# Retention followed by a multiplicative feed-forward layer: five moves in the order of transposes, state products and loads

## The chip, the cores and the metric

The kernel runs on one core of one Trainium2 chip. TensorE (PE, with its weight loads listed apart as PEld), VectorE (DVE), ScalarE (ACT) and GpSimd (POOL) each work through their own instruction list in program order; SyncE (SP) issues the transfers. The metric is the device time of one execution in microseconds, lower is better. Before the change seven executions have a median of 184.77 us (183.8 to 185.63).

## The reference

Inputs q, k and v are float32 of 4 batches x 8 heads x 768 positions x 64; the weights are w1 and w2 (512 x 1024), w3 (1024 x 1024) and w_out (1024 x 512). The output is 3072 x 512, float32.

```python
gamma = 1.0 - 2.0 ** (-5.0 - np.arange(H))          # one decay for each head
for t in range(S):
    state = gamma * state + outer(k[:, :, t], v[:, :, t])
    y[:, :, t] = q[:, :, t] @ state / sqrt(D)
x = y.transpose(0, 2, 1, 3).reshape(B * S, H * D)    # 3072 x 512
out = ((x @ w1) * (x @ w2)) @ w3 @ w_out
```

## The kernel before

**The mathematics as tiled.** The recurrence is cut into chunks of 128 positions: within a chunk, masked scores of queries and keys times the values (`intra`), and a product of the queries with the state before it (`inter`); the state itself is carried on with a product of keys and values (`kv`) and a decay. The decays are put into scalings of the values (`VS`), the outputs (`YS`) and the state (`GS`). All of these matmuls are 64 x 64 tiles in float16. The product w3 @ w_out is formed once (`W3O`), so that a chunk's feed-forward part is two products with W1 and W2 (`ab(f)`, f from 0 to 7: `a_unit`, four matmuls copied out of PSUM by ACT, and `b_unit`, four matmuls multiplied by that on DVE into `HT`) and two output blocks `o_unit(e)` of eight matmuls of 512 columns each.

**Stages.** The instruction order on each engine is the order of the program text (a manual schedule). At the start the weights arrive; `w3_transpose`, `w3_part` and `W3Block` (its eight matmuls are issued in portions by `mm(n)`, its result goes out by `back()`) form `W3O`. Meanwhile the first 256 positions of two batches are handled by two objects `Pairs`, b0 and b1, and W1 and W2 are cast to float16 as they land (`cast_w` and single copies). The first feed-forward block f0 is done by weight rows (`by_rows`), so that each W tile is used when it is there; `f1` fills in between. Then come steps m = 2 to 11 (so the "third step" is m = 2, the "fourth" m = 3, the "tenth" m = 9), each for one chunk of a pair of batches: `step2()` for m = 2, `step(m)` after it. A step holds the attention part of chunk m, the outputs of chunk m-1 and the feed-forward of chunk m-1 and m-2.

**Keys and queries, transposed.** The scores want keys and queries with the head dimension on partitions. Queries from step 4 on are transposed by transfers that SP issues (`q_dma`). Keys are transposed either on PE (`k_transposes`: eight 128 x 128 transposes into one PSUM bank and a DVE copy) or by such a transfer (`k_dma`); the set `K_PE` = (3, 5, 8) names the steps m in which the next step's keys go through PE.

**The order in a step before.** In `step(m)` for m > 4 the small matmuls stand together: `intra(m-1)`, `kv(m)`, `scores(m)`, `inter(m-1)`, the last held behind a one-element mark on ACT (`ended`) since two row halves add to one bank. For m in `EARLY` the `intra` stands earlier, among the `ab`. For m = 3 and 4 the order is another: step 3 has `inter(2)` and `scores(3)`, and later, among the `ab`, `intra(3)` and `kv(3)`; step 4 has `inter(3)`, `kv(4)`, `scores(4)`. After the group come, on DVE, the outputs of chunk m-1 (`outputs_back`, three operations), the evacuations of the state products (`kv_back`), and the masks on the scores (`am_back`).

**Memory that sets waits.** PSUM has eight banks: X0, X1, Y0, Y1 by name, and four in rotation (`ps_f`) for everything called psF, psO, psW and psK. Loads land in 22 staging tiles in rotation; the loads of q, k and v for steps 2 to 4 are issued at the top of the program in the order of the text, the later ones in the steps.

Of the kernel before, what the change touches and what calls it, by code (L numbers as in the profile page):

```python
# [18 lines left out]
def kernel(  # L19
# [11 lines left out]
    nc = tc.nc  # L31
# [9 lines left out]
    TB = 256  # L41
    K_PE = 4

# [43 lines left out]
    def load_k(m):  # L87
        load_kv(m, k_in, k)

    def load_v(m):  # L90
        load_kv(m, v_in, v)
# [39 lines left out]
    w1_st = [load_rows(moe_w1, d) for d in range(4)]  # L131
# [2 lines left out]
    load_q(3)  # L134
    for m in range(2, 5):
        load_k(m)
        if m == 3:
            load_q(4)
            load_q(5)
        load_v(m)  # L140

    Z = const.tile([128, 512], HP, name="zeros")
    nc.vector.memset(Z[:, :].bitcast(FP), 0.0)  # L143
# [136 lines left out]
    def q_cast(n, *engs):  # L280
        if n not in q_in:
            return
        q16s[n] = att.tile([128, 1024], HP, tag="q16", name="q16", bufs=2)
        pairs_cast(q16s[n], q_in.pop(n), *engs)
# [21 lines left out]
    def v_cast(m, engs):  # L306
        v16 = att.tile([128, 2, 512], HP, tag="v16", name="v16", bufs=3)
        v32 = v_in.pop(m)
        for e, eng in enumerate(engs):
            eng.tensor_tensor(  # L310
                v16[:, e, :].rearrange("j (h d) -> j h d", d=D),
                v32[:, e, :].rearrange("j (h d) -> j h d", d=D),
                VS[:, 2, :].unsqueeze(2).broadcast_to((128, H, D)),
                MULT,
            )
        v16s[m] = v16
# [19 lines left out]
    def q_dma(n):  # L336
        if n not in q16s:
            return
        qT = att.tile([128, 2, NP, 128], HP, tag="qT", name="qT", bufs=5)
        nc.sync.dma_start_transpose(  # L340
            qT[:, :, :, :].rearrange("p t a i -> p (t a) i"), q16s.pop(n)[:, :]
        )
        qTs[n] = qT
# [5 lines left out]
    def k_transposes(m, tag):  # L349
        k16, kT = k16s[m], new_kT(m)  # L350
        if tag:
            ps = bank(tag, [128, 2, NP, 128], HP, "psTk")
        else:
            ps = ps_f.tile([128, 2, NP, 128], HP, tag="psF", name="psTk")
        for e in range(2):
            for p in range(NP):
                nc.tensor.transpose(ps[:, e, p, :], k16[:, e, p * 128 : (p + 1) * 128], ident16[:, :])  # L357
        nc.vector.tensor_copy(
            kT[:, :, :, :].rearrange("p e a j -> p (e a j)"), ps[:, :, :, :].rearrange("p e a j -> p (e a j)")
        )  # L360
# [36 lines left out]
    class Pairs:  # L397
# [59 lines left out]
        def kv(self, psf):  # L457
            if psf:
                self.s = [ps_f.tile([128, NP, L], FP, tag="psF", name="psK") for s in range(2)]
            else:  # L460
                self.s = [bank(f"X{s}", [128, NP, L], FP, "psK") for s in range(2)]
            for p in range(NP):
                for t in range(2):
                    for s in range(2):
                        for r in range(2):
                            c0 = p * 128 + r * 64
                            nc.tensor.matmul(
                                self.s[s][half(r), p, :],
                                lhsT=self.k16[half(s), t * 512 + c0 : t * 512 + c0 + 64],
                                rhs=self.v16[half(s), t, c0 : c0 + 64],  # L470
                                start=(p == 0 and t == 0), stop=(p == NP - 1 and t == 1),
                            )
# [33 lines left out]
        def outputs_back(self, s):  # L506
            if self.e not in XT:
                XT[self.e] = xpool.tile([128, NP * 2, 2, L], HP, tag="xt", name="xt")
            nc.vector.tensor_tensor(
                XT[self.e][:, :, :, :].rearrange("p (a s) b x -> p a s (b x)", s=2)[:, :, s, :]  # L510
                .rearrange("p a (b i t) -> p a t b i", b=2, t=2),
                self.y[s][:, :, :].rearrange("p a (t b i) -> p a t b i", t=2, b=2),
                YS[:, 0:2, :, :].rearrange("p b a (t i) -> p a t b i", t=2), MULT,
            )
# [107 lines left out]
    class Ffn:  # L622
# [27 lines left out]
            ps = self.mm(W2, f)  # L650
            nc.vector.tensor_tensor(self.HT[:, f, :], self.pa.pop(f)[:, :], ps[:, :], MULT)  # L651

        def o_unit(self, e, parts=((0, 512),), store=True):
            bp, c = divmod(self.m, NCH)
            osb = fsb.tile([128, DM], FP, tag="osb", name="osb", bufs=4)
            r0 = (bp * 2 + e) * S + c * C if self.m > 1 else self.m * S + e * C
            for c0, c1 in parts:
                cs = slice(c0, c1)
                psO = ps_f.tile([128, c1 - c0], FP, tag="psF", name="psO")
                for f in range(8):  # L660
                    nc.tensor.matmul(  # L661
                        psO[:, :], lhsT=self.HT[:, f, e * 128 : (e + 1) * 128], rhs=W3O[f][:, cs],
                        start=(f == 0), stop=(f == 7),
                    )
                nc.scalar.activation(osb[:, cs], psO[:, :], AF.Copy, scale=final_scale)  # L665
                if store:
                    (nc.sync if self.m < NSTEP - 1 else nc.scalar).dma_start(out[r0 : r0 + 128, cs], osb[:, cs])
            return lambda: nc.sync.dma_start(out[r0 : r0 + 128, :], osb[:, :])
# [6 lines left out]
    def cast_w(W, st, d, on_dve):  # L675
        cast_to(W[d][:, :], st[d][:, :], on_dve)
# [46 lines left out]
    wb = W3Block(4)  # L723
# [5 lines left out]
    wb = W3Block(5)  # L729
# [4 lines left out]
    b0, b1 = Pairs(0), Pairs(1)  # L734
    b0.k_cast(nc.vector)
    q_transposes(0, "Y0", False)
    b0.k_transposes("Y1", True)
    b0.v_cast(nc.gpsimd, 0)
    b0.v_cast(nc.gpsimd, 1)
    wb = W3Block(6)  # L740
    wb.mm(4)
    am_back = b0.scores(0)
    am_back(0)
    am_back(1)
    wb.mm(4)
    wb.back()
    wb = W3Block(7)
    am_back = b0.scores(1)
    am_back(0)
    b0.kv(True)  # L750
# [15 lines left out]
    nc.scalar.copy(W1[0][:, 0:512], w1_st[0][:, 0:512])  # L766
    nc.gpsimd.tensor_copy(W1[0][:, 512:1024], w1_st[0][:, 512:1024])
    b1.v_cast(nc.gpsimd, 1)
    wb.mm(2)
    am_back = b1.scores(0)  # L770
    am_back(0)
    am_back(1)
    wb.mm(4)
    wb.back()
    cast_w(W1, w1_st, 1, False)
    b0.next_state_decay()
    nc.gpsimd.tensor_copy(W1[2][:, :], w1_st[2][:, :])
    nc.scalar.copy(W1[3][:, 0:512], w1_st[3][:, 0:512])
# [62 lines left out]
    for f in range(2):  # L841
        f1.ab(f)
    q_transposes(3, "Y0", False)
    stores = [f0.o_unit(0, store=False)]
    k_transposes(2, "Y1")
    f1.ab(2)

    def step2():
        am_back = scores(2)
        am_back(0)  # L850
        am_back(1)
        stores.append(f0.o_unit(1, store=False))
        k_cast(3, (nc.gpsimd, nc.scalar))
        for n in (4, 5):
            q_cast(n, nc.gpsimd)
        for n in (4, 5):
            q_dma(n)
        for store in stores:
            store()
        for f in range(3, 5):  # L860
            f1.ab(f)
        intra(2)
        kv_back = kv(2, True)
        kv_back(0)
        f1.ab(5)
        k_transposes(3, None)
        f1.ab(6)
        kv_back(1)
        v_cast(3, (nc.gpsimd, nc.gpsimd))
        f1.ab(7)  # L870

    EARLY = (6, 11, 12)

    K_PE = (3, 5, 8)

    def step(m):

        kv_backs = []  # L880
        if m > 4:
            last = None if m in EARLY else ended(intra(m - 1))
            if m < NSTEP:
                kv_backs.append(kv(m, True))
                am_back = scores(m)
            inter(m - 1, last)
        else:
            inter(m - 1)
            if m == 4:
                kv_backs.append(kv(m, True))  # L890
            am_back = scores(m)
        outputs_back(m - 1, 0)
        outputs_back(m - 1, 1)
        if m >= NSTEP:
            return
        if m + 1 < NSTEP:
            k_cast(m + 1, (nc.gpsimd, nc.gpsimd))
            if m not in K_PE:
                k_dma(m + 1)
        for kv_back in kv_backs:  # L900
            kv_back(0)
            kv_back(1)
        am_back(0)
        am_back(1)
        ffn[m - 2].o_unit(0)
        ffn[m - 2].o_unit(1)
        load_q(m + 3) if m % 2 == 0 else None
        load_k(m + 2)
        load_v(m + 2)
        load_q(m + 3) if m % 2 else None  # L910
        for f in range(2):
            ffn[m - 1].ab(f)
        if m + 1 in EARLY:
            intra(m)
        if m + 1 < NSTEP:
            v_cast(m + 1, (nc.gpsimd, nc.gpsimd))
        if m == 3:
            intra(m)
            kv_back = kv(m)
            kv_back(0)  # L920
        ffn[m - 1].ab(2)
        ffn[m - 1].ab(3)
        if m == 3:
            kv_back(1)
        if m % 2 == 0:
            for n in (m + 2, m + 3):
                q_cast(n, nc.gpsimd)
            for n in (m + 2, m + 3):
                q_dma(n)
        for f in range(4, 8):  # L930
            if f == 6 and m in K_PE:
                k_transposes(m + 1, None)
            ffn[m - 1].ab(f)
# [42 lines left out]
```

## Time and profile before

| what | value |
|---|---|
| median of 7 executions | 184.77 us |
| the profiled execution, its own time | 184.4 us |
| its span in the profile | 182.5 us |
| TensorE's granted clock, mean | 1.00 |
| matmuls, PE | 2642 |
| from HBM, read and written | 29.36 MB and 6.29 MB |
| mean duration of a 128 x 256 product with W1 or W2 on PE | 273 ns (x672) |
| mean duration of one output matmul of 512 columns on PE | 380 ns (x184) |
| mean duration of one key transpose on PE | 219 ns (x40) |
| DVE copy of eight transposed blocks | 691 ns (x5) |
| POOL, scaling one half of a step's values | 1044 ns (x20) |
| one transpose of keys by SP's queue: time on SP, time to landing | 1.24 to 2.43 us, 3.1 to 5.2 us (x5) |

A duration on PE is that of one matmul from start to end; matmuls follow one another before the one ahead has ended, so the distance between two starts is what a row of them costs. In the chain of waits each piece is listed with its start, its length and what it is; in the timeline each row has the start, the length, the engine and line, and in brackets how long the engine was idle before it and what ended that. A weight load on PEld belongs to the matmul that follows it.

### The profile page before, as it was taken

What the parts mean: (1) busy time and instruction counts of PE and PEld (TensorE: products, weight loads), DVE (VectorE), ACT (ScalarE), POOL (GpSimd) and SP (SyncE); (2) the same over time, 40 slices, a digit from 0 to 9 for tenths busy, and PEclk for the clock granted to TensorE, in tenths of its full rate; (3) what the DMA queues carried; (4) which work ended last, traced back from release to release, by engine and by line L of the source; (5) the groups of instructions that cost most, each with busy time, mean ns of one, the idle gap of its engine ahead of it and who ended that gap; (6) DMA issues with size and microseconds to landing.
All of it is one profiled execution on the core that took longest, in us unless ns stands there. A gap on an engine that the chain in (4) does not pass through costs nothing.

```text
span 182.5 us, 6235 instructions
## 1 busy us (share of the span) xinstructions
PE 175.7 (96%) x2642; PEld 125.2 (69%) x2642; DVE 109.4 (60%) x205; ACT 72.1 (39%) x156; POOL 71.0 (39%) x126
## 2 busy tenths in 40 slices
PE   7889989999999999999999999999999999999992
PEld 2445646588756795885877858769678587685872
DVE  2247668660669678649377493595684856846330
ACT  4353836565720342433424415243244242442532
POOL 3127536764547741824426364147362160000000
PEclk9999999999999999999999999999999999999999
DMA  5999999999999998999999999999999910200203
GB/s 207 355 418 403 299 288 347 403 374 245 206 274 223 164 304 179 200 306 203 216 224 200 307 171 243 199 243 251 170 170 271 166 66 4 115 0 22 96 0 115
DMA packets 78474, 39.44 MB, mean 216 GB/s; under 512 B 56304, under 2 KB 72944, under 8 KB 78448
## 3 DMA queue, kind: packets, MB, share of 16 engines
q1 hardware_dynamic: 78016, 38.54, 88.6%
q8 instruction: 20, 0.33, 0.8%
q10 hardware_dynamic: 432, 0.52, 0.8%
q14 instruction: 6, 0.05, 0.1%
HBM read 29.36 MB, written 6.29 MB: 195 GB/s over the span
## 4 chain that ended last, share of the span: by engine, by line
PE 78%; SPq 9%; DMA 8%; ACT 2%; issue 0%; DVE 0%; ACTq 0%
PE psF L636 40%; PE psO L661 23%; SPq L63 9%; DMA stg<-in_moe_w_out_dram 5%; DMA stg<-in_moe_w_dram 4%; PE psF L791 3%; PE psY L531 2%; PE psA L383 2%; PE psY L599 2%; PE psG L636 2%; PE psK L551 2%; PE psTk L357 1%; ACT w L220 1%; PE psTq L328 0%; ACT osb L665 0%
## 5 line engine op out<-in xcount | busy, mean ns | idle before, releaser
L636 PE MATMUL psF<-xt,w 128*128 128x256 f16 x672 | 77.0, 273 | 0.0
L636 PEld LDWEIGHTS <-w 128*128 128x128 f16 x704 | 68.2, 98 | 10.3
L651 DVE TENSOR_TENSOR ht<-pa,psF 128x256 f16<-128x256 f32 x88 | 36.9, 420 | 37.3 <-PE psF L636 31.7
L645 ACT COPY pa<-psF 128x256 f32<-128x256 f32 x80 | 29.8, 372 | 38.0 <-PE psF L636 38.0
L661 PE MATMUL psO<-w3o,ht 128*128 128x512 f16 (+2 forms) x200 | 43.7, 371 | 0.0
L661 PEld LDWEIGHTS <-ht 128*128 128x128 f16 x200 | 18.5, 98 | 19.7
L665 ACT ACTIVATE osb<-psO 128x512 f32<-128x512 f32 (+2 forms) x25 | 14.5, 580 | 44.2 <-PE psO L661 44.2
L614 DVE TENSOR_TENSOR xt<-psY,YS 64x512 f16<-64x512 f32 (+1 forms) x29 | 21.0, 726 | 4.4 <-PE psY L599 4.1
L310 POOL TENSOR_TENSOR v<-stg,VS 128x512 f16<-128x512 f32 x20 | 20.6, 1044 | 5.3 <-DMA stg<-in_v_dram 5.2
L303 POOL CAST k<-stg 128x512 f16<-128x512 f32 x18 | 11.1, 614 | 23.1 <-DMA stg<-in_k_dram 22.8
L290 POOL CAST q<-stg 128x1024 f16<-128x1024 f32 (+1 forms) x12 | 12.1, 1005 | 15.3 <-DMA stg<-in_q_dram 11.4
L566 POOL TENSOR_TENSOR t<-s,GS 128x512 f16<-128x512 f32 x8 | 8.3, 1041 | 14.5 <-DVE s L565 14.5
L390 DVE TENSOR_TENSOR am<-psA,keep 128x512 f16<-128x512 f32 x20 | 12.8, 682 | 0.3 <-PE psA L383 0.2
L791 PE MATMUL psF<-xt,w 128*128 128x256 f16 x64 | 8.5, 273 | 0.3
L248 DVE COPY w3t<-psW 128x1024 f16<-128x1024 f16 x8 | 5.5, 690 | 5.3 <-PE psW L244 5.3
L255 PE MATMUL psW<-wo,w3t 128*128 128x512 f16 x32 | 7.9, 386 | 0.6 <-ACT wo L224 0.5
L269 PE MATMUL psW<-wo,w3t 128*128 128x512 f16 x32 | 8.4, 381 | 0.0
L684 PE MATMUL psZ<-zeros 128*128 128x512 f16 (+1 forms) x18 | 6.6, 504 | 1.3 <-DVE zeros L143 1.3
L791 PEld LDWEIGHTS <-w 128*128 128x128 f16 x64 | 5.8, 98 | 2.2 <-ACT w L220 0.7
L573 DVE TENSOR_TENSOR t<-psK,t 128x512 f16<-128x512 f32 x9 | 6.2, 690 | 0.8 <-PE psK L551 0.6
L244 PEld LDWEIGHTS <-w3h 128*128 128x128 f16 x64 | 4.4, 103 | 3.2 <-DVE w3h L231 1.7
L225 POOL CAST wo<-stg 128x512 f16<-128x512 f32 x4 | 2.5, 615 | 10.2 <-DMA stg<-in_moe_w_out_dram 10.2
(90 smaller groups left out, 149.7 us busy)
## 6 DMA issues: line engine op xcount, KB each, us to landing
stg<-in_moe_w_dram SPq DMA_DIRECT2D x16, 512.0 KB, 9.0
stg<-in_q_dram SPq DMA_DIRECT2D x12, 512.0 KB, 6.2
out_dram<-osb SPq DMA_DIRECT2D x22, 256.0 KB, 3.1
stg<-in_k_dram SPq DMA_DIRECT2D x20, 256.0 KB, 5.8
stg<-in_v_dram SPq DMA_DIRECT2D x20, 256.0 KB, 5.6
stg<-in_moe_w_out_dram SPq DMA_DIRECT2D x4, 512.0 KB, 7.9
stg<-in_k_dram SPq DMA_DIRECT2D x2, 512.0 KB, 9.9
stg<-in_v_dram SPq DMA_DIRECT2D x2, 512.0 KB, 8.6
```

Source lines behind the costliest of these rows:

```text
L63: nc.sync.dma_start(dst, src)
L290: (nc.scalar.copy if eng is nc.scalar else eng.tensor_copy)(dst[:, :].rearrange("i (t h d) -> i h t d", t=2, d=D)[:, hs, :, :], src[:, :]. ...
L303: (nc.scalar.copy if eng is nc.scalar else eng.tensor_copy)(dst, src)
L310: eng.tensor_tensor(v16[:, e, :].rearrange("j (h d) -> j h d", d=D), v32[:, e, :].rearrange("j (h d) -> j h d", d=D), VS[:, 2, :].unsqueez ...
L390: nc.vector.tensor_tensor(am[:, r, :, :], ps[r][:, :, :], keep[:, :].unsqueeze(1).broadcast_to((128, NP * 2, L)), MULT,)
L614: nc.vector.tensor_tensor(XT[m][to, :, s, :].rearrange("p (a e) (i t) -> p a e t i", e=2, t=2), psYs[m][s][fr, :, :].rearrange("p (a e) (t ...
L636: nc.tensor.matmul(ps[:, :], lhsT=W[d][:, f * 128 : (f + 1) * 128], rhs=self.x(d), start=(d == 0), stop=(d == 3),)
L645: nc.scalar.copy(self.pa[f][:, :], ps[:, :])
L651: nc.vector.tensor_tensor(self.HT[:, f, :], self.pa.pop(f)[:, :], ps[:, :], MULT)
L661: nc.tensor.matmul(psO[:, :], lhsT=self.HT[:, f, e * 128 : (e + 1) * 128], rhs=W3O[f][:, cs], start=(f == 0), stop=(f == 7),)
L665: nc.scalar.activation(osb[:, cs], psO[:, :], AF.Copy, scale=final_scale)
L791: nc.tensor.matmul(ps[f // 2][:, f % 2, :], lhsT=W[d][:, f * 128 : (f + 1) * 128], rhs=f0.x(d), start=(d == 0 and f % 2 == 0), stop=(d == ...
```

## The change

Five things are moved or replaced.

1. **Loads.** In the list at the top the values of step 3 are loaded ahead of the queries 4 and 5.
2. **The start.** b0's key transposes stand between the two halves of `W3Block(6)`, whose result goes out before the masks; three of `W3Block(7)`'s matmuls stand ahead of the second scores, and correspondingly fewer later. W1's second tile is cast half by ACT and half by POOL, not by ACT alone.
3. **The third step.** Its key transposes are issued inside the first output block of f0, after four of its eight matmuls (`between`), where they stood after the block; `f1.ab(2)` goes behind the second output block.
4. **The fourth step.** `kv(3)` stands with `inter(2)` and `scores(3)`, its two results in the rotating banks and evacuated with the outputs; `intra(3)` moves into step 4, whose group has the four kinds of the later steps. To have the values in time, their cast stands ahead of the query casts in `step2`; the casts, the transposing transfers of queries 4 and 5 and the two stores go behind `kv_back(1)`.
5. **The tenth step.** `K_PE` loses its 8: the keys of m = 9 are transposed by a transfer.

```diff
     for m in range(2, 5):
         load_k(m)
+        load_v(m)
         if m == 3:
             load_q(4)
             load_q(5)
-        load_v(m)
...
-        def o_unit(self, e, parts=((0, 512),), store=True):
+        def o_unit(self, e, parts=((0, 512),), store=True, between=None):
...
                 for f in range(8):
+                    if f == 4 and between:
+                        between()
                     nc.tensor.matmul(
...
-    b0.k_transposes("Y1", True)
     b0.v_cast(nc.gpsimd, 0)
     b0.v_cast(nc.gpsimd, 1)
     wb = W3Block(6)
     wb.mm(4)
+    b0.k_transposes("Y1", True)
+    wb.mm(4)
     am_back = b0.scores(0)
+    wb.back()
     am_back(0)
     am_back(1)
-    wb.mm(4)
-    wb.back()
     wb = W3Block(7)
+    wb.mm(3)
     am_back = b0.scores(1)
...
-    wb.mm(2)
+    wb.mm(1)
     am_back = b1.scores(0)
     am_back(0)
     am_back(1)
-    wb.mm(4)
+    wb.mm(2)
     wb.back()
-    cast_w(W1, w1_st, 1, False)
+    nc.scalar.copy(W1[1][:, 0:512], w1_st[1][:, 0:512])
+    nc.gpsimd.tensor_copy(W1[1][:, 512:1024], w1_st[1][:, 512:1024])
...
-    stores = [f0.o_unit(0, store=False)]
-    k_transposes(2, "Y1")
-    f1.ab(2)
+    stores = [f0.o_unit(0, store=False, between=lambda: k_transposes(2, "Y1"))]
 
     def step2():
         am_back = scores(2)
...
         stores.append(f0.o_unit(1, store=False))
         k_cast(3, (nc.gpsimd, nc.scalar))
-        for n in (4, 5):
-            q_cast(n, nc.gpsimd)
-        for n in (4, 5):
-            q_dma(n)
-        for store in stores:
-            store()
-        for f in range(3, 5):
+        v_cast(3, (nc.gpsimd, nc.gpsimd))
+        for f in range(2, 5):
             f1.ab(f)
         intra(2)
...
         kv_back(1)
-        v_cast(3, (nc.gpsimd, nc.gpsimd))
+        for n in (4, 5):
+            q_cast(n, nc.gpsimd)
+        for n in (4, 5):
+            q_dma(n)
+        for store in stores:
+            store()
         f1.ab(7)
...
-    K_PE = (3, 5, 8)
+    K_PE = (3, 5)
 
     def step(m):
 
         kv_backs = []
-        if m > 4:
+        if m > 3:
             last = None if m in EARLY else ended(intra(m - 1))
             if m < NSTEP:
                 kv_backs.append(kv(m, True))
...
         else:
             inter(m - 1)
-            if m == 4:
-                kv_backs.append(kv(m, True))
             am_back = scores(m)
+            kv_backs.append(kv(m, True))
...
-        if m == 3:
-            intra(m)
-            kv_back = kv(m)
-            kv_back(0)
         ffn[m - 1].ab(2)
         ffn[m - 1].ab(3)
-        if m == 3:
-            kv_back(1)
```

## The prediction

> **What bounds the kernel.** I read the page first, then the busy time by stretch, then the chain of waits in order of time, and last the timeline around each edit.
>
> ```profile
> span 182.5 us, 6235 instructions
> PE 175.7 (96%) x2642; PEld 125.2 (69%) x2642; DVE 109.4 (60%) x205; ACT 72.1 (39%) x156; POOL 71.0 (39%) x126
> PEclk9999999999999999999999999999999999999999
> ```
>
> ```profile
> 33.20:46.10 12.90, 12.71 (x184) 10.26 (x185) 5.60 (x11) 7.18 (x14) 8.25 (x10) 1.00 1.05 330
> 46.10:57.30 11.20, 10.85 (x243) 7.83 (x241) 7.88 (x16) 4.52 (x7) 5.56 (x7) 1.00 1.13 241
> 57.30:70.00 12.70, 12.70 (x252) 9.65 (x248) 9.47 (x19) 4.07 (x10) 7.34 (x8) 1.00 1.21 233
> 70.00:175.80 105.80, 105.80 (x1658) 79.69 (x1650) 67.63 (x128) 38.16 (x96) 35.08 (x40) 1.00 0.83 170
> ```
>
> The columns after the stretch are its length, then busy time of PE, PEld, DVE, ACT and POOL. From 57.3 to 175.8 us PE is never idle, at full granted clock: there only fewer or denser matmuls shorten the kernel. Before 57 us PE has holes, and a hole is worth its length only if PE, not a transfer or cast, sets what comes next. The chain shows one true hole and the work that two other edits touch:
>
> ```profile
> 49.77 0.46 PE psTk L357 x8
> 50.23 0.02 issue
> 50.25 0.70 DVE kT L358
> 50.95 0.04 issue
> 51.00 0.45 PE psA L383 x32
> ...
> 62.66 0.38 PE psY L531 x32
> 63.03 0.26 PE psK L551 x31
> ...
> 126.65 0.45 PE psTk L357 x8
> ```
>
> The sum is made against the profiled execution: span 182.5, its own time 184.4. The seven runs have a median of 184.77; I subtract the gain from that.
>
> **Third step's transposes (gain 0.41 us).** The eight transposes of step 2's keys start at 49.60, DVE's copy ends at 50.94, the scores start at 51.00: 1.40 us from first transpose to scores. Between lie the transposes (8 at 0.056 between starts, 0.45) and unit 2 (4 at 0.109, 0.44): a hole of 0.51, of which 0.09 is what PE takes anyway when it goes from 128x128 to 64x64 matmuls (the last start before each such group is 0.203 ahead of the first of it, not 0.109). After, the transposes come four output matmuls earlier, at 48.74, with four more (4 x 0.216 = 0.86) behind them: PE is through at 50.05 and could start the scores at 50.15; the copy (50.25 less 0.86 = 49.39, DVE idle since 48.43) allows 50.14. The keys' casts end at 48.29 (ACT 47.67 + 0.62), so they aren't waited for. Scores at 50.15 instead of 51.00, with the 0.44 of unit 2 still to do: 0.85 - 0.44 = 0.41. If the copy were a DVE operation (0.42) late, the gain would be near 0; it can't exceed 0.51.
>
> **Fourth step's small matmuls in one group (gain 0.15 us).** Now steps 3 and 4 hold three groups of 64x64 matmuls: previous-state and scores, 56.52 to 57.28; values and state products apart, 62.50 to 63.23; three kinds, 68.93 to 70.03: 0.76 + 0.73 + 1.10 = 2.59 with entry and exit. After: one of three (1.10) and one of four, as in the later steps (116.44 to 117.79, 1.35; 1.28 to 1.39 elsewhere). 2.59 - 2.45 = 0.14 to 0.15; 0.10 to 0.21 by the spread. The new `ended` mark on ACT waits for 32 matmuls while PE has kv and scores to do, 0.6 us; where this form already runs PE shows no hole.
>
> What moves with it: kv(3) runs at about 56.8 instead of 62.9, so step 3's values must be cast by then. They landed at 57.0 and 58.1 (issued at 50.76 and 52.25, 6.2 and 5.9 to landing); now they go ahead of two query loads that landed at 53.9 and 55.8. With k's second half landing at 52.1 (47.19 + 4.9) and a half every 1.15, I estimate 53.3 and 54.4; POOL, which sat idle 2.48 us before 54.09, casts them (1.04 each) by 55.5. Margin 1.3 us. The query casts go behind them and the state's decay and end near 60.2, before the first key cast at 60.52 and before SP, busy issuing loads until 59.6, gets to the second query transpose (62.49). DVE gets two evacuations (0.69 + 0.68) in step 3 ahead of the masks. In step 4 the same list ends its second 4.25 us after its group starts; in step 3 DVE begins its outputs 1.08 after the group, not 0.53, so 4.80; the product that reuses that bank starts at 73.94 - 69.02 = 4.92. I charge nothing, by 0.12 us. If DVE is one such operation (0.69) later, PE waits 0.57.
>
> The Trainium skill (TensorEngine Tiling, PSUM Bottleneck) speaks against this part: tiling speeds up matmuls but not PSUM evacuation, so DVE could become the limit. By that rule the 0.57 would be paid and the sum be 0.48; the step 4 rows say the four banks absorb it.
>
> **Tenth step's keys by the queue (gain 0.45 us).** Eight transposes at 126.65 leave PE: 0.45 by the chain, and 0.44 by the steps' own pitch (116.53 to 128.78 is 12.25 with them, 104.74 to 116.53 is 11.79 without, 128.78 to 140.61 is 11.83). DVE loses a copy of 0.69, off the path. SP gains one transpose DMA behind key casts that end at 119.75. It occupies SP for 1.24 to 2.43 and lands 3.1 to 5.2 after issue: by 125, or behind the last queued load (123.7) about as late; scores(9) want it at 128.7. Behind it in SP's queue wait two stores (issued 120.35 and 122.07, set by ACT), one query, two key and two value loads, two query transposes and step 10's keys: at most about 1 us later. The nearest is step 10's keys, landing at 137.4, wanted at 141.1 less my 1.05: slack about 1.7 after the delay. Stretch 70 to 175.8 has a DMA share of 0.83, so there is room.
>
> The Trainium skill (TensorE: Matmul & The Clock Gate, Part 4: PE-mode transpose) gives about 275 ns for such a transpose in a kernel; eight would be 2.2 us and the time 182.0. The rows are 219 ns for one, but 56 ns between starts; the overlap decides.
>
> **First keys' transposes and W1's second tile (gain 0.04 us).** PE waits 0.63 us before 24.46 for the keys' cast; four row products (0.87) now fill that. But see what follows:
>
> ```profile
> 32.51 0.62 ACT L766 CAST w<-stg 128x512 f16<-128x512 f32 x1 [0.52 <-DMA stg<-in_moe_w_dram]
> 33.17 0.33 PEld L791 LDWEIGHTS <-w 128*128 128x128 f16 x4 [0.59 <-ACT w L766]
> 34.17 1.29 DVE L436 TENSOR_TENSOR am<-psA,keep_t 128x512 f16<-128x512 f32 x2 [0.74 <-PE psA L429]
> 35.01 0.33 PEld L791 LDWEIGHTS <-w 128*128 128x128 f16 x4 [0.37 <-ACT w L220]
> 35.55 0.26 PEld L450 LDWEIGHTS <-v 64*64 64x64 f16 x16 [0.21 <-issue]
> ```
>
> The first W1 product at 33.18 waits for a cast that itself waited for a transfer, and no transfer before it is moved. Products done earlier only lengthen the wait there. Nor is it reached late: scores(0) shift from 25.88 to about 26.15, the second batch about 0.27 later through the mask bank, the second keys' transposes (POOL's cast ends 30.20) from 30.25 to 30.36; two products fewer remain after b1's scores, so PE arrives near 32.5, 0.7 early. ACT's half of W1's second tile takes 0.62 instead of 1.04, so its matmuls run at 34.74 and not 35.01. But b1's intra needs the second mask, done at 35.46, and began at 35.55: 0.04 is all. POOL's half (0.62) pushes the state decay to 35.3 and W1's third tile to end at 36.35; that one is wanted at 37.09. Bounds: 0.25 gained if the mask gives way too, 0.3 lost if POOL's casts come late; taken 0.04, which the mask row says.
>
> **Sum.** 0.41 + 0.15 + 0.45 + 0.04 = 1.05 us: 184.77 - 1.05 = 183.7 (183.35 for the profiled execution).
>
> **Rivals.**
> (a) DVE in step 3 is late, or the scores of step 2 wait for the copy: half of the gain goes. Price 0.57: 184.3. For: a margin of 0.12; against: four banks in rotation. Chance 0.19.
> (b) The opening gains too, W1's landing coming earlier than this trace has it so that the filled 0.63 counts: 183.1. For: PE is near 0.7 early; against: loads follow one another at 1.2 to 1.4 us whatever PE does. Chance 0.10.
> (c) Slower: step 3's values aren't there when kv(3) wants them. If they landed at 57.0 and 58.1 as now, casts end at 59.2 and PE stands 2.4 us at 56.8: 184.77 + 2.4 - 1.05 = 186.1. It decides from a landing of the second half after 55.7; each microsecond beyond costs one. For: SP's issue there is already throttled, over 1 us each; against: 3.7 us of query loads move behind them. Chance 0.09.
> (d) The forecast: 0.62.
>
> **How the numbers follow.** A measurement of this kernel tells about 0.5% from no change: below 183.85 is faster, above 185.69 slower. The forecast's own range is 183.3 to 184.1; about three quarters of it is under 183.85: 0.47 faster, 0.15 same. With (b) faster is 0.57, with (a) same is 0.34, (c) slower 0.09. The range takes in (a) and most of (b), and leaves out (c): 182.9 to 184.7.
>
> **What would show it.** Right: scores(2) start within 0.1 us of their entry pause; one group of four kinds in step 4 and none alone in step 3; no key transposes on PE between steps 8 and 9; the first W1 product still at about 33.2 with a longer wait. Wrong: a PE wait on POOL's value cast near 56.8, on DVE near 61, or on a transpose DMA near 128.5 or 140.

## The result, and the profile after

Slower by 1.35%: the changed kernel took 187.98 us (median of 25 executions, 185.46 to 192.17) against 184.73 us before (62 executions); the ratio is 1.0135, 95% interval 1.0108 to 1.0162. The ratio is lower than the quotient of the medians (1.0176) because it leaves out executions that were more than 1.5% above the fastest of their kernel. The forecast was 183.7 us, within 182.9 to 184.7. The profiled execution took 187.08 us. Its page, opening lines, the slices with the granted clock, and the queue that carries instructions:

```profile
span 185.0 us, 6222 instructions
...
PEclk9999999999998799999999999999999999999999
...
q8 instruction: 20, 0.33, 0.8%
```

The clock has two slices below full, 55.5 to 64.8 us. Before it had none. The last line says that 20 packets with 0.33 MB went to instruction lists, 16 KB each; remember it. Busy time by stretch (columns as in the prediction: length, then PE, PEld, DVE, ACT, POOL, then granted clock, DMA share, GB/s):

```profile
45.40:55.40 10.00, 10.00 (x177) 7.13 (x175) 7.19 (x15) 4.73 (x7) 5.93 (x7) 1.00 1.09 224
55.40:70.00 14.60, 12.09 (x171) 8.38 (x171) 8.35 (x17) 3.32 (x8) 7.58 (x9) 0.88 1.04 229
70.00:178.10 108.10, 108.10 (x1785) 81.70 (x1783) 68.92 (x131) 39.02 (x99) 35.03 (x40) 1.00 0.85 170
```

Ahead of step 3's group PE has no hole (there it had 0.35 us of holes in 11.2), and behind 70 us none. The whole loss lies between: 14.60 - 12.09 = 2.51 us in which PE stands, and a clock of 0.88. The chain of waits, in order of time, shows where:

```profile
48.13 0.45 PE psTk L357 x8
48.58 0.86 PE psO L663 x4
49.44 0.38 PE psA L383 x32
...
55.50 0.38 PE psY L599 x32
55.88 0.29 PE psA L383 x31
56.17 0.13 PE psK L551 x13
56.30 2.51 issue
58.81 0.48 PE psK L551 x16
59.29 4.98 PE psO L663 x16
...
71.70 0.38 PE psY L531 x32
72.08 0.26 PE psK L551 x30
72.34 0.32 PE psA L383 x32
72.66 0.29 PE psY L599 x32
```

Three things are to be seen. The first three pieces are the third step's edit as drawn: transposes, four output matmuls, scores, with nothing between. The last four are step 4's group of four kinds in one row, 1.25 us. And in step 3's group PE stops in the middle of `kv(3)`, after 13 of its 32 matmuls, for 2.51 us, and the chain calls it "issue": PE waits for nothing that the profile shows. The 16 output matmuls behind the stop take 4.98 us; at their pitch of 0.216 they would take 3.46. That is the halved clock: it was at 0.5 for 3.41 us, from the last tenth of a microsecond of the stop on, and the first of these matmuls stand up to 0.427 apart.

Two things end about when PE stops or starts, and both look guilty. Timeline of the same kernel:

```profile
53.65 2.04 POOL L310 TENSOR_TENSOR v<-stg,VS 128x512 f16<-128x512 f32 x2 [1.84 <-PE psK L551]
...
56.52 2.19 DVE L614 TENSOR_TENSOR xt<-psY,YS 128x512 f16<-128x512 f32 x3
```

POOL's values are cast by 55.69, 0.3 us before `kv(3)`'s first matmul, so that they can't stop its 14th; DVE's outputs end at 58.71, 0.1 us before PE goes on. A `kv` matmul needs no output of DVE, though, but a bank of PSUM, and it had two: by the program's text the 13 matmuls had gone into both in turn, and the 14th goes to the first of them again. What remains as the likeliest is that PE had no instructions.

**How PE gets them.** The packets of the instruction queue stand in the trace with start and end; here they are laid beside PE's list. A matmul is two rows of it (weight load and matmul), a semaphore instruction one more. Counted so, PE's stop is at row 1472 here, and the stops of all the runs below are at rows 704, 1472, 3264, 3520 and 4032 (to within a row or two): the distances are multiples of 256. A packet of 16 KB is thus taken to be 256 rows of 64 bytes; 20 packets are 5120 rows, and PE's list has some 5280. As 1472 = 6 x 256 - 64, the blocks below start at rows of that form:

```
kernel   block of rows  PE runs it, us    next packet, us   PE goes on   after packet's end
before   1216 to 1471   54.36 to 60.10    56.39 to 57.66    60.10        2.44 (no stop)
after    1216 to 1471   53.17 to 56.11    56.31 to 57.32    58.81        1.49
after    3264 to 3519   117.11 to 120.35  117.64 to 118.81  120.35       1.54 (no stop)
```

The last row is a block nearly as short that made no stop: its packet came 0.53 us after it began.

The packet for the next block comes at about the time when PE takes up the block ahead of it, mostly after: in the changed kernel it began 3.14 us after the block did (2.03 before), took 1.01, and PE went on 1.49 after its end. A block that PE uses up sooner than the sum of the three ends in a stop. Before, this block lasted 5.74 us, since its last 13 matmuls were output matmuls, at 0.216 for two rows. After, `kv(3)`, whose 32 matmuls take 0.3 us, stands ahead of them, so that the 256 rows hold no output matmul and last 2.94.

### The profile page after: what moved, and what is told of

Read it like the earlier page. It is cut to its first block, busy times and chain, and to the rows that moved or that the text cites. A ratio compares the mean times of both kernels' runs of the same rounds, so it can differ in the third digit from the quotient of the medians.

```text
span 185.0 us, 6222 instructions
## 1 busy us (share of the span) xinstructions
PE 175.6 (95%) x2634; PEld 125.0 (68%) x2634; DVE 108.8 (59%) x204; ACT 72.0 (39%) x157; POOL 71.5 (39%) x127
## 4 chain that ended last, share of the span: by engine, by line
PE 78%; SPq 9%; DMA 8%; issue 2%; ACT 1%; ACTq 0%
PE psF L636 40%; PE psO L663 23%; SPq L63 9%; DMA stg<-in_moe_w_out_dram 4%; PE psF L795 4%; DMA stg<-in_moe_w_dram 4%; PE psY L531 2%; PE psA L383 2%; PE psK L551 2%; PE psG L636 2%; PE psY L599 2%; PE psTk L357 1%; ACT w L220 1%; PE psTq L328 0%; ACT osb L667 0%
## 5 line engine op out<-in xcount | busy, mean ns | idle before, releaser
L663 PE MATMUL psO<-w3o,ht 128*128 128x512 f16 (+2 forms) x200 | 45.3, 379 | 0.0
L551 PE MATMUL psK<-v,k 64*64 64x64 f16 x288 | 4.7, 197 | 2.5 <-issue 2.5
L686 PE MATMUL psZ<-zeros 128*128 128x512 f16 (+1 forms) x18 | 5.9, 460 | 1.3 <-DVE zeros L143 1.3
L255 PEld LDWEIGHTS <-w3t 128*128 128x128 f16 x32 | 3.0, 97 | 4.7 <-issue 1.1
```

The costliest lines, as they stand in the source:

```text
L663: nc.tensor.matmul(psO[:, :], lhsT=self.HT[:, f, e * 128 : (e + 1) * 128], rhs=W3O[f][:, cs], start=(f == 0), stop=(f == 7),)
```

## The experiments

The theory: PE's list ran dry at a block boundary (A). The rivals: the values or their casts hold `kv(3)` (B); DVE or a PSUM bank holds it (C); chance of one execution (D). The expectations call (A) theory S, (B) theory V and (C) theory D.

**The changed kernel again.** No edit.

> The changed kernel once more, as the yardstick of this group. Theory S (supply of instructions): PE's instructions come in blocks of 16 KB, 256 rows of its list, each fetched when the block before the last begins; in the changed kernel one block's rows (1216 to 1471) are used up in 2.9 us and PE stands at row 1472, amid kv(3). So the stop should recur at the same place, after 13 of the 32 matmuls of kv(3), some 1.5 us after the end of the 16 KB instruction packet that goes before it, whatever POOL and DVE do then; 2 to 3 us long; ratio 1.010 to 1.017. Theory V (values late): a stop before the 17th matmul, ending within 0.1 us of POOL's second value cast. Theory D (DVE): a stop that ends within 0.15 us of a DVE operation, as it did in the first profile (58.70 against 58.81).

Ratio 1.0098 (1.0073 to 1.0124), median 189.26 over 6 executions, with 186.39 for the profiled one. The stop is at the same instruction again, after 13 matmuls, and takes 2.90 us between starts (2.70 the first time); the packet ran from 56.92 to 58.11, PE went on at 59.63, 1.52 after it. So (D), chance, falls. DVE's outputs ended at 59.32 here, 0.31 us before PE went on, not 0.1. In this execution the clock didn't drop: behind the stop the output matmuls stand 0.216 apart.

```profile
56.61 0.31 PE L551 MATMUL psK<-v,k 64*64 64x64 f16 x13
...
59.63 0.35 PE L551 MATMUL psK<-v,k 64*64 64x64 f16 x19 [2.71 <-issue]
59.91 1.47 PE L663 MATMUL psO<-w3o,ht 128*128 128x512 f16 x6
```

**The blocks shifted by 112 rows.** The zero products at the start, which write a bank that nothing reads, are cut into smaller ones with about the same time on PE: 56 matmuls more, and nothing else moves.

```diff
-    busy(8)
+    busy(38, n=108)
...
-    busy(2, n=400)          # twice
+    busy(6, n=133)
...
-    busy(3)                 # twice
+    busy(12, n=128)
```

> The changed kernel with the zero products of the opening cut into more and smaller ones of the same sum: 56 more matmuls (112 rows of PE's list), no work of PE longer, nothing else touched. Theory S: every block boundary moves 112 rows ahead in the program, the shortest blocks then last 3.6 us (near 102 us) and 4.0 us (near 124); no stop at kv(3), nor a drop of the clock; 183.3 to 184.2 us, about 1.0 us below the kernel before, ratio 0.993 to 0.997. Theories V and D: the opening changes nothing for kv(3); ratio 1.010 to 1.017 as the changed kernel.

Ratio 0.9993 (0.997 to 1.0016), median 184.33: the loss is gone, with every wait on values, DVE and banks left as it was. The gain that was expected (0.993 to 0.997) isn't there, for a new stop came, in a place where the shortest block had been put at 3.6 us and thought long enough:

```profile
57.30 0.47 PE L551 MATMUL psK<-v,k 64*64 64x64 f16 x32
57.70 3.63 PE L663 MATMUL psO<-w3o,ht 128*128 128x512 f16 x16
...
107.54 1.67 PE L663 MATMUL psO<-w3o,ht 128*128 128x512 f16 x7 [0.60 <-issue]
```

`kv(3)` runs through, 32 in a row. At 106.56 PE now stops among output matmuls: two starts are 0.98 us apart and not 0.216, so that 0.77 are lost. That block began at 103.36, its packet ran from 104.69 to 105.97, and PE went on 1.57 after that. A stop follows the block, not the kind of matmul.

**The blocks of the kernel before, shifted by 48 rows.** If (A) holds, a kernel without the change can be made to stop.

```diff
-    busy(8)
+    busy(32, n=128)
```

> The kernel before, with its first eight zero products of 512 columns cut into 32 of 128: 24 more matmuls (48 rows), the same PE time. Theory S: the boundaries now fall so that the block near 54 us lasts 2.9 us and the one near 128 us 1.6 us; two stops of 1.5 to 3 us, near 57 and 130, each perhaps with a drop of the clock behind it; 188 to 192 us, ratio 1.02 to 1.04. Theories V and D: nothing that kernel waits for has moved; 184.4 to 185.1, ratio 0.998 to 1.002.

Ratio 1.0117 (1.009 to 1.0143), median 186.88. Slower with no other edit, by stops in three places: 1.27 us in the opening's `intra` at 33.4, 1.55 among the scores of step 3 and 1.16 among the `inter` in step 9:

```profile
57.31 0.35 PE L383 MATMUL psA<-qT,kT 64*64 64x64 f16 x21
...
59.03 0.28 PE L383 MATMUL psA<-qT,kT 64*64 64x64 f16 x11 [1.37 <-issue]
...
133.00 0.22 PE L599 MATMUL psY<-qT,t 64*64 64x64 f16 x4 [0.97 <-issue]
```

PE went on 1.42, 1.43 and 1.65 us after the ends of the packets (33.22, 57.60 and 131.36). The loss is less than expected (1.02 to 1.04): the later two packets came 1.70 and -0.12 us after their blocks began (below zero: while the block before was still running), against 3.14 in the changed kernel. The lag isn't a constant.

**Values that are there long before.** `kv(3)` takes the values of step 2 in place of those of step 3, so that the states after step 3, and the output from them, differ.

```diff
-        k16, v16 = k16s[m], v16s[m]
+        k16, v16 = k16s[m], v16s[2 if m == 3 else m]
```

> The changed kernel with kv(3) taking the values of step 2, cast some 4 us earlier, in place of those of step 3 (the states after step 3 are therefore other ones; the number and shape of the operations stay). Theory S: the stop stays where it is, after 13 matmuls of kv(3), and the time too: ratio 1.010 to 1.017. Theory V: no stop, 183.3 to 184.2. Theory D: the stop stays.

```profile
56.62 2.19 DVE L614 TENSOR_TENSOR xt<-psY,YS 128x512 f16<-128x512 f32 x3
...
58.28 0.35 PE L551 MATMUL psK<-v,k 64*64 64x64 f16 x19 [1.87 <-issue]
```

Ratio 1.0079 (1.0036 to 1.0122), a little under the expected 1.010 to 1.017. The stop is at the same row with nothing to wait for, 2.06 us long (packet 55.78 to 56.79, PE on at 58.28, 1.49 behind). (B) falls. So does DVE as the releaser: its outputs end at 58.81, 0.53 us after PE has gone on.

**The change without the fourth step's part.** The loads, casts and order of steps 2 to 4 as before; the opening, the third step and the tenth as changed.

```diff
-        if m > 3:
+        if m > 4:
...
+        if m == 3:
+            intra(m)
+            kv_back = kv(m)
+            kv_back(0)
```

> The change without its part on the fourth step (and so without the new order of step 3's loads and casts): the opening, the third step's transposes and the tenth step's keys alone. Theory S: the rows of the dense groups stand as in the kernel before (only 16 fewer from step 8 on), so no stop for instructions longer than 0.3 us; the terms 0.41 + 0.45 + 0.04 show whole: 0.9 us below the kernel before, ratio 0.993 to 0.998. If instead one of the other parts carries the loss (rival: the transposes between the output matmuls, or the tenth step's transfer on SP's queue), ratio over 1.003.

```profile
56.61 0.46 PE L383 MATMUL psA<-qT,kT 64*64 64x64 f16 x32
57.01 3.63 PE L663 MATMUL psO<-w3o,ht 128*128 128x512 f16 x16
```

Ratio 0.9954 (0.9921 to 0.9988), median 184.17 against 185.01. No stop. The other three parts together are worth what they were priced at; the loss comes only with the fourth.

**The shift by 112 rows, and step 7's `intra` early.** The stop that the shift made at 106.56 is taken away by spreading that step's group: its `intra` goes among the `ab`, as in steps 6, 11 and 12.

```diff
-    EARLY = (6, 11, 12)
+    EARLY = (6, 7, 11, 12)
```

> The changed kernel with the 112 added rows, and step 7's values product (intra(6)) put among the feed-forward products of step 6, as steps 6, 11 and 12 have it: 64 rows leave the group at 105 us, before which the run with 112 rows stood 0.77 us. Theory S: that stop goes, at the price of one more group (0.21 us); between the first output matmul and the last step's 127.77 (before) - 1.05 + 0.2 = 126.9 us; 183.4 to 184.1 us, ratio 0.993 to 0.998. If the 0.77 were a wait of another kind, it stays and the group's price comes on top: ratio 0.998 to 1.003.

```profile
span 181.4 us, 6332 instructions
...
105.19 3.63 PE L663 MATMUL psO<-w3o,ht 128*128 128x512 f16 x16
```

Ratio 0.9897 (0.9852 to 0.9941), median 183.56 against 185.01: no stop, 126.82 us from the first output matmul to the last step's outputs (127.77 before), faster than both kernels, with the whole change in it. It is near an edge, too: at 128.41 PE took up a block 1.66 us after its packet's end.

**The shift, with step 3's values loaded late.** The loads at the top in the old order, the rest as in the shift by 112. This brings about the prediction's slower rival (c).

```diff
     for m in range(2, 5):
         load_k(m)
-        load_v(m)
         if m == 3:
...
+        load_v(m)
```

> The changed kernel with the 112 added rows and the loads in their old order: step 3's values behind the queries 4 and 5. This is the slower rival of the prediction by itself: the values land at about 57.0 and 58.1, are cast by 58.1 and 59.2, and kv(3), wanted at about 56, waits before its first or its 17th matmul until then: 2 to 3 us, ended by POOL's casts (not by an instruction packet). Theory S has nothing against it; the place of the stop and what ends it are to show how the two kinds of wait look apart. 186 to 188.5 us.

```profile
59.24 0.32 PE L551 MATMUL psK<-v,k 64*64 64x64 f16 x16 [2.19 <-POOL v L310]
60.25 0.32 PE L551 MATMUL psK<-v,k 64*64 64x64 f16 x16 [0.69 <-POOL v L310]
```

Two executions, 188.21 and 191.46, no interval. The values landed at 58.01 and 59.09, and PE waited twice, 2.36 + 0.88 = 3.24 us beyond the usual distance of its starts, each time named as POOL's cast. This is how rival (c) looks: a named releaser, at the first and the 17th matmul, where a half of the values begins. The changed kernel's stop has no releaser and stands at the 14th. (An instruction stop of 1.27 us at 109.36 came on top.)

(C) was not tried by an edit of its own; but a bank or DVE would hold `kv(3)` in the shifted kernel too, where nothing does, and with the old values PE went on before DVE's outputs had ended.

## Why the prediction was wrong, point by point

The measure is the time from the first output matmul of f0 to the last step's outputs, which leaves out the arrival of the weights (the first W1 product ran at 33.18 before, at 32.46 after, by the transfers). Before 127.77 us. The prediction's three terms in it make 0.41 + 0.15 + 0.45 = 1.01.

```
kernel                 terms      stops      clock     sum      measured
after                  -1.01      +2.70      +1.48     130.94   130.90
the same again         -1.01      +2.90       0        129.66   129.58
shift 112              -1.01      +0.77       0        127.53   127.43
without fourth step    -0.86       0          0        126.91   126.88
values of step 2       -1.01      +2.30       0        129.06   128.96
values loaded late     -1.01      +4.51       0        131.27   131.15
```

Stops are taken between starts, less the usual distance of these. With the values of step 2 a second, small stop of 0.24 us at 118.27 is in the sum; with the values loaded late the 3.24 us behind POOL's casts are. The clock's term is seven starts at up to 0.427 and not 0.216 apart, 1.43 in all, and 0.05 where the group ends. All sums hold within 0.12 us. So the terms that were forecast were paid, and the loss is a term that wasn't in the sum.

- **Third step, 0.41.** Right. The scores start at 49.37, 0.09 past their place in the row of output matmuls, which is the entry pause; before it was 0.51. Without the fourth step's part the gain is 127.77 - 126.88 = 0.89, against 0.41 + 0.45 for this and the tenth step.
- **Tenth step, 0.45.** Right in the same sum; PE waits for no transfer near 128.5 or 140.
- **Opening, 0.04.** Right: from the first W1 product to the first output matmul 14.65 us, before 14.70, and 14.65 or 14.66 in five of the six experiments with the changed opening (14.92 in the repetition). Rival (b), an earlier W1, stays undecided: the first W1 product ran at 33.18 and 32.48 in the two traces with the old opening and at 32.46 to 33.77 in the seven with the new one.
- **Fourth step, gain of 0.15.** As far as it went, right: with stops and clock taken off and the 0.89 of the kernel without it, the five rows above that have it leave 0.16 to 0.24 for it. Here is the step that failed, and it failed by an omission: "where this form already runs PE shows no hole", and so the group in step 3 was charged nothing. That row of evidence was true of the later steps and says nothing of this place, since a hole of this kind depends on where the block boundary falls and not on the form of the group. The missing term is 2.7 us in which PE waits for its instructions, and in most executions 1.5 us of halved clock behind it.
- **The values.** Right: landed at 53.5 and 54.6 (estimated 53.3 and 54.4), cast by 55.69 (55.5). Rival (c) had the sign, the group of matmuls and, by chance, nearly the size (2.4), but not the mechanism; without the load's move it would have come, at 3.2 us rather than 2.4.
- **DVE's margin of 0.12**, and the PSUM warning weighed there: no wait of PE on DVE appears after the group. The stop gave DVE 2.7 us more there; but in the run shifted by 112 rows, where `kv(3)` runs through, PE has no hole behind it either (products follow at 61.16, at their usual distance).

Could it have been seen? The profile of before has the instruction queue on its page, and its trace has the packets. The block from 114.26 to 117.50 lasted 3.24 us, and the next was taken up 1.72 us after its packet's end, where stops end 1.30 to 1.65 after: a kernel without a hole was 0.1 to 0.4 us from one. With the fourth step's group in place, counting rows gives a block of some 2.9 us at a point where the packet had come 2.03 us late.

## What to carry to other kernels

Where small matmuls are brought together, count PE's instructions as well as its time: 256 rows used up in less than some 5.6 us (3.1 for the packet to start, 1.0 for it, 1.5 to go on, as here at 53 us) may end in a stop that no semaphore explains; later in the program, where packets came sooner, blocks of 3.24 us did without one. Keep matmuls of 512 columns between dense groups, or shift the blocks with harmless rows ahead, and look at every block afterwards, since a shift moves all of them. In a profile, "issue" on a busy engine's chain in the middle of a uniform group of matmuls is to be laid beside the instruction queue's packets before any data wait is blamed.

## What the hardware showed that wasn't expected

- **Only one block ahead.** Over these traces packets began from 2.1 us before to 4.6 us after the start of the block in front of theirs, and took 0.88 to 2.36 us. In all ten stops timed this way (the eight told above, the 0.24 us with the values of step 2, and 0.40 us at 32.25 in the opening of the run shifted by 112 rows) PE went on 1.30 to 1.65 us after the packet's end. Blocks begun before 60 us had a mean lag of 2.25 us, later ones 1.04. The DMA share of the changed kernel was 1.09 and 1.04 in the two stretches before 70 us and 0.85 after; that the loads make the lags long was not tried and stays open.
- **The clock.** A stand of 2.70 us was followed by 3.41 us at half clock in one execution, one of 2.90 us in another by none. Such a stretch makes a mean granted clock of 0.991 over the span; of 26 executions of the changed kernel 18 are at 0.991 or below and 8 at 0.997 or above, while the kernel before (37 executions) and the run shifted by 112 rows (12) never fall below 0.997. The Trainium skill (TensorE: Matmul & The Clock Gate, Part 1) says that the clock is halved after at least one idle window of about 3.4 us and that this window runs freely. The length of 3.41 agrees; that 2.70 us of idling were enough does not, and why one execution was hit and the other spared was not settled here.
